# Four PSUM banks of two score tiles taken anew as four tiles of one bank, in an attention and MLP kernel

## The chip, the core and the metric

The kernel runs on one core of a Trainium2 chip. The metric is the device time of one execution in microseconds, and the median over several executions is compared. TensorE (PE, with its weight loads as PEld), VectorE (DVE), ScalarE (ACT), GpSimd (POOL) and SyncE (SP) each work through an instruction list of their own in order. They wait for each other on semaphores. TensorE writes its products to PSUM, which has eight banks; DVE and ACT read them from there.

## What is computed

Attention with RMS-normalised q and k, followed by an MLP over the tokens of all heads:

```python
# q, k, v: (8, 12, 448, 64); w_in: (768, 2048); w_out: (2048, 768)
q_n, k_n = rmsnorm(q, g_q), rmsnorm(k, g_k)
attn = softmax(q_n @ k_n^T / 8)
x = (attn @ v).transpose(0, 2, 1, 3).reshape(3584, 768)
h = x @ w_in
out = (h * sigmoid(1.702 * h)) @ w_out          # (3584, 768), float32
```

## The kernel before

**Attention.** A unit of work is a pair of heads of one batch: 6 pairs in each of 8 batches. `score` (L1170) multiplies k by q for a block of 112 keys into a score tile of PSUM; `expo` (L1178, L1180) takes the exponential on ACT; `values` (L1191) multiplies by v into a tile `o`; `divide` (L1201, L1202) normalises on DVE, and a transpose puts the result as columns of x into `xT`.

**PSUM.** Eight banks are shared out at the start. Two score tiles `sc0` and `sc1` have two banks each, one for each head of the pair, since one `exp` reads both. The tile `o` has one bank, and `w0`, `w1`, `w2` have one each. A list `banks` names what the matrix products may write to: places 0 to 2 are the `w` tiles, and places 3 to 6 are the single banks within the score tiles. These four lines make it (L1008 to L1010 and L1014):

```python
banks = [ps_w.tile([128, 512], FP32, tag=f"w{j}", name=f"w{j}") for j in range(3)]
sc_ring = [ps_sc.tile([128, 2, 512], FP32, tag=f"sc{j}", name=f"sc{j}") for j in range(2)]
banks += [t[:, j, :] for t in sc_ring for j in range(2)]
...
return banks[od.got]
```

**The MLP.** For batches 0 to 5, `first` (L1403) multiplies by `w_in`, `tanh` (L1413) and `gate` (L1425) make the activation, and the product with `w_out` follows (L1433 plain, L1497 in a form with seven products for every eight, whose operands are sums made on DVE at L1488). A product's result is taken out of PSUM by ACT (`copy_out`, L1507), or added to an earlier part by DVE (`add_out`, L1515). The first product of the last two batches is made jointly, again with seven products in place of eight: `joint_product` (L1744) writes three matmuls for each of the seven into a bank, ACT or DVE copies a part out (`part_copy`, L1755 and L1753), DVE adds later parts (`part_add`, L1758), and `gelu` (L1764) makes the activation on ACT. Its operand differences are made on DVE at L1728 and L1734.

**The order.** The kernel has no loop at run time. Every step is added to a planner (`_Order`) with an engine, an assumed duration, a key, the steps it depends on and the PSUM slot that it takes. The planner plays the steps through by these assumed durations and emits each engine's instructions in the order found. A slot named "w" stands for a place in `banks`; it has 3 places until the step "late" (L1842), which depends on the last `exp` and widens it to all 7. Steps with engine "none" emit no instruction of their own. Tile places and waits are made below this level: the waits between engines come from which tiles the instructions read and write.

Of the kernel before, what the change touches and what calls it, by code (L numbers as in the profile page):

```python
# [9 lines left out]
FP32 = mybir.dt.float32  # L10
# [5 lines left out]
PSUM = bass.MemoryType.PSUM  # L16
# [841 lines left out]
def kernel(  # L858
# [31 lines left out]
    def pool(name, bufs, **kw):  # L890
        return ctx.enter_context(tc.tile_pool(name=name, bufs=bufs, **kw))
# [43 lines left out]
    late = consts.tile([128, 3 * T_LEN + N_SUM * S_LEN], BF16, name="late", tag="late")  # L935
# [58 lines left out]
    for t in att_ring[1:]:  # L994
        flat = t[:, :, :, :].rearrange("p n h q -> p (n h q)").bitcast(FP32)
        osb_ring += [flat[:, j * S:(j + 1) * S] for j in range(NS)]
    ps_sc = pool("ps_sc", 1, space=PSUM)
    ps_o = pool("ps_o", 1, space=PSUM)
    ps_w = pool("ps_w", 1, space=PSUM)

    od = _Order()
    for name, n in (("sc", 2), ("o", 1), ("w", 2), ("th", 3), ("osb", 5)):
# [5 lines left out]
    banks = [ps_w.tile([128, 512], FP32, tag=f"w{j}", name=f"w{j}") for j in range(3)]  # L1008
    sc_ring = [ps_sc.tile([128, 2, 512], FP32, tag=f"sc{j}", name=f"sc{j}") for j in range(2)]
    banks += [t[:, j, :] for t in sc_ring for j in range(2)]  # L1010
    scored = [0]

    def bank():
        return banks[od.got]  # L1014
# [243 lines left out]
    def last_values(i):  # L1258

        return [("P", i, None, w, NS - 1) for w in range(2)] + [("P", i, h, 0, NS - 1)  # L1260
                                                                for h in range(2)]
# [8 lines left out]
    for i in range(NG):  # L1270
        b = i // NP
# [57 lines left out]
    for u in units:  # L1329
        i, h = u  # L1330
        b = i // NP
# [193 lines left out]
    def now_key():  # L1525
        return 10.3 + min(done, TURN) / PACE + max(done - TURN, 0.0) / PACE_2
# [198 lines left out]
    def w_term(j, h):  # L1725
        o, x, y, op = W_TERMS[j]
        o, x, y = (t[:, :, h * FH // 2:(h + 1) * FH // 2] for t in (o, x, y))
        nc.vector.tensor_tensor(out=o, in0=x, in1=y, op=op)  # L1728

    def x_term(j):  # L1730
        o, x, y = ((X1, x_half(B1, 0), x_half(B0, 0)),
                   (x_half(B1, 0), x_half(B1, 1), x_half(B1, 0)),
                   (X2, x_half(B1, 1), X1), (X4, x_half(B0, 1), X2))[j]
        nc.vector.tensor_tensor(out=o, in0=x, in1=y, op=ALU.subtract)  # L1734
# [79 lines left out]
    for b in range(B - 1):  # L1814
        bp = b // 2
        if b == B - 2:
            b = B - 1
# [19 lines left out]
        if b == B0 - 1:  # L1837
            od.add("keep", "DVE", 650, keep, now_key() + 0.5, lock=True,
                   deps=[("G", B0 - 2, m) for m in range(MI)]
                   + [x for p in range(NG - 2) for x in last_values(p)])  # L1840
            before_g.append("keep")
            od.add("late", "none", 0, lambda: None, 0, widen=[("w", len(banks))],  # L1842
                   deps=[("E", NG - 1, None, t) for t in range(NS)])
            od.add("later", "none", 0, lambda: None, 0,
                   widen=[("osb", len(osb_ring)), ("sums", len(sums))],
                   deps=last_values(NG - 1))
            for j in range(4):
                for h in range(2):
                    od.add(("WT", j, h), "DVE", 960, lambda j=j, h=h: w_term(j, h),
                           now_key() + 1.5 + j / 10, lock=True,  # L1850
                           deps=[last] + [("WT", i, h) for i in range(j)]
                           + [x for p in range(NG - K_RAW, NG)
                              for x in (("N", p, 0), ("N", p, 1), ("V", p))])
            for j, d in enumerate(((0, 1), (1,), (1,), (0,))):
                od.add(("XT", j), "DVE", 860, lambda j=j: x_term(j), now_key() + 2.0 + j / 10,
                       lock=True,
                       deps=[("XT", i) for i in range(j)]
                       + [("X", (B0 + e) * NP + p, None) for e in range(2) for p in range(NP)
                          if j or p < KH]
                       + [x for p in range(NG - K_RAW, NG)  # L1860
                          for x in (("N", p, 0), ("N", p, 1), ("V", p))])
# [73 lines left out]
```

## Time and profile before

| what | before |
|---|---|
| median of 4 runs | 424.08 us (423.62 to 426.0) |
| the profiled execution | 423.85 us |
| its span, first to last instruction | 422.1 us |
| PE busy | 404.8 us, 96% |
| DVE busy | 324.3 us, 77% |
| ACT busy | 295.4 us, 70% |
| POOL busy | 173.5 us, 41% |
| mean DMA rate | 150 GB/s |
| granted TensorE clock | 1.0 throughout |

The busy times are of one profiled execution, and all times within it count from the start of its span. Matmuls overlap: a row of three matmuls at L1744 reads 0.73 us, while the next group can start 0.57 us after it. So a stall on PE is read from the starts of neighbouring groups and not from the idle time between them. A trace names both banks of a score tile `sc`. In the timeline neighbouring instructions of one engine and line are merged ("x3"), and a bracket at the end of a row tells how long the engine had been idle and what ended it.

### The profile page before, as it was taken

The numbers are of one execution on the slowest core, as the hardware profiler recorded it, in microseconds if no ns is written. First come the engines' busy times: TensorE is split into PE (matmuls) and PEld (weight loads), VectorE is DVE, ScalarE is ACT, GpSimd is POOL, SyncE is SP. The second block draws the span as 40 slices with busy tenths as digits, with TensorE's granted clock in tenths as the row PEclk, the third lists the DMA queues.
The fourth block names the chain that finished last, engine by engine and source line by source line (L and its number), as shares of the span: only waits on it lengthen the run. The fifth ranks groups of instructions, "written<-read, shape, count | busy, mean of one in ns | idle before, by whom it ended". The sixth has DMA issues, their size and how long they took to land.

```text
span 422.1 us, 10002 instructions
## 1 busy us (share of the span) xinstructions
PE 404.8 (96%) x3845; PEld 237.6 (56%) x3845; DVE 324.3 (77%) x647; ACT 295.4 (70%) x435; POOL 173.5 (41%) x252
## 2 busy tenths in 40 slices
PE   7899989999999999999999999999999999999995
PEld 5568876555555555554555555555555654545663
DVE  4878888869999788888798869997666897557432
ACT  4898595989788578776896758858887625773221
POOL 4965887571726175809447363752300000000000
PEclk9999999999999999999999999999999999999999
DMA  8999999965394899695875879558351231001223
GB/s 214 254 245 245 259 249 248 242 171 130 78 191 119 187 206 227 121 230 132 205 174 119 196 182 231 122 111 181 93 110 36 74 77 43 3 0 27 87 76 112
DMA packets 101555, 63.38 MB, mean 150 GB/s; under 512 B 54916, under 2 KB 101508, under 8 KB 101508
## 3 DMA queue, kind: packets, MB, share of 16 engines
q1 hardware_dynamic: 93712, 55.88, 56.4%
q0 software_dynamic: 7296, 6.29, 9.1%
q8 instruction: 30, 0.49, 0.5%
q10 hardware_dynamic: 500, 0.57, 0.4%
q14 instruction: 17, 0.14, 0.1%
HBM read 45.61 MB, written 11.01 MB: 134 GB/s over the span
## 4 chain that ended last, share of the span: by engine, by line
PE 67%; DVE 13%; DMA 12%; ACT 3%; issue 2%; SPq 1%; POOL 0%; DVEq 0%; ACTq 0%; POOLq 0%
PE w L1403 19%; PE w L1497 18%; PE o L1191 9%; DMA rows<-in_v_dram 8%; PE sc L1170 8%; PE sc L1497 5%; PE w L1433 4%; DMA w_out_s<-in_moe_w_out_dram 3%; PE sc L1744 2%; DVE ssq L1058 2%; PE w L1744 2%; DVE late L1488 1%; DMA rows<-in_k_dram 1%; DVE obs L1202 1%; DVE att L1758 1%
## 5 line engine op out<-in xcount | busy, mean ns | idle before, releaser
L1178 ACT ACTIVATE att<-sc 112x896 bf16<-112x896 f32 x168 | 146.0, 917 | 35.7 <-PE sc L1170 35.0
L1403 PE MATMUL w<-xt,w_in_s 128*128 128x448 bf16 (+1 forms) x672 | 120.7, 326 | 0.6 <-DVE g L1425 0.4
L1403 PEld LDWEIGHTS <-w_in_s 128*128 128x128 bf16 x672 | 61.0, 98 | 44.6 <-issue 9.9
L1191 PEld LDWEIGHTS <-att 112*128 112x128 bf16 x1536 | 62.6, 98 | 29.8 <-issue 8.2
L1100 POOL TENSOR_TENSOR row<-rows,rs 112x512 bf16<-112x512 f32 x61 | 66.7, 1115 | 11.0 <-DMA qk<-row 9.1
L1413 ACT ACTIVATE th<-w 128x448 f32<-128x448 f32 x96 | 51.9, 548 | 23.4 <-PE w L1403 22.5
L1425 DVE SCALAR_TENSOR_TENSOR g<-th,w 128x448 bf16<-128x448 f32 x96 | 57.9, 615 | 12.9 <-ACT th L1413 12.6
L1058 DVE TENSOR_REDUCE ssq<-sq 112x16 f32<-112x1024 f32 (+1 forms) x50 | 58.3, 1170 | 10.0 <-ACT sq L1049 8.2
L1191 PE MATMUL o<-vx,att 112*128 112x65 bf16 x1280 | 58.8, 194 | 3.9 <-DVE obs L1202 3.0
L1113 POOL TENSOR_TENSOR vx<-rows,ones 112x512 bf16<-112x512 f32 x20 | 21.8, 1092 | 66.4 <-PE o L1191 58.6
L1170 PE MATMUL sc<-qk 64*128 64x448 bf16 (+1 forms) x360 | 47.3, 342 | 0.4 <-DVE qk L1130 0.2
L1046 POOL TENSOR_TENSOR sq<-rows 112x1024 f32<-112x1024 f32 (+1 forms) x14 | 26.8, 1914 | 42.1 <-DMA rows<-in_k_dram 18.8
L1202 DVE TENSOR_TENSOR obs<-o,rcp 112x256 bf16<-112x256 f32 x96 | 40.8, 425 | 3.3
L1497 PEld LDWEIGHTS <-g 128*128 128x128 bf16 x296 | 27.2, 98 | 21.1 <-issue 4.7
L1497 PEld LDWEIGHTS <-late 128*128 128x128 bf16 x304 | 27.5, 97 | 19.2 <-issue 2.9
L1049 ACT ACTIVATE sq<-rows 112x1024 f32<-112x1024 f32 (+1 forms) x32 | 32.4, 1018 | 6.8 <-DMA rows<-in_k_dram 4.1
L1497 PE MATMUL w<-w_out_s,g 128*128 128x384 bf16 x152 | 28.7, 326 | 0.0
L1497 PE MATMUL w<-w_out_s,late 128*128 128x384 bf16 x152 | 28.6, 326 | 0.0
L1201 DVE RECIPROCAL rcp<-o 112x4 f32<-112x4 f32 x96 | 17.0, 177 | 14.3 <-PE o L1191 14.0
L1497 PE MATMUL w<-late 128*128 128x384 bf16 x128 | 24.2, 326 | 0.1
L1100 DVE TENSOR_TENSOR row<-rows,rs 112x512 bf16<-112x512 f32 x27 | 22.5, 834 | 2.0 <-POOL rs L1093 2.0
L1180 ACT ACTIVATE att<-sc 112x896 bf16<-112x896 f32 x24 | 20.5, 917 | 1.4 <-PE sc L1170 1.3
(130 smaller groups left out, 503.5 us busy)
## 6 DMA issues: line engine op xcount, KB each, us to landing
rows<-in_q_dram SPq DMA_DIRECT2D x44, 224.0 KB, 4.6
rows<-in_k_dram SPq DMA_DIRECT2D x43, 224.0 KB, 4.7
rows<-in_v_dram SPq DMA_DIRECT2D x42, 224.0 KB, 3.5
w_in_s<-in_moe_w_in_dram POOLq DMA_DIRECT2D x4, 768.0 KB, 16.7
w_out_s<-in_moe_w_out_dram POOLq DMA_DIRECT2D x4, 768.0 KB, 20.8
out_dram<-osb SPq DMA_DIRECT2D x10, 168.0 KB, 3.4
out_dram<-osb SPq DMA_DIRECT2D x14, 120.0 KB, 2.2
out_dram<-osb SPq DMA_DIRECT2D x11, 144.0 KB, 2.5
```

The lines of the kernel that those rows point to most:

```text
L1046: nc.gpsimd.tensor_tensor(out=sq[i % N_SQ][:SS, part], in0=raw[turn(i, N_RAW, K_RAW)][:SS, part], in1=raw[turn(i, N_RAW, K_RAW)][:SS, part ...
L1049: nc.scalar.activation(out=sq[i % N_SQ][:SS, part], in_=raw[turn(i, N_RAW, K_RAW)][:SS, part], func=ACT.Square)
L1058: nc.vector.reduce_sum(out=ssq_of[g0][:SS, i - g0, part], in_=sq[i % N_SQ][:SS, part], axis=AX.X)
L1100: eng.tensor_tensor(out=row_ring[i % N_QKN][:SS, gi].rearrange("p n (h d) -> p h n d", h=2), in0=raw[turn(i, N_RAW, K_RAW)][:SS, gi], in1= ...
L1170: nc.tensor.matmul(sc[:, hp, j * SH:j * SH + n], lhsT=qkw[r, k0:k0 + WIN], rhs=qk[r, 0, qs], start=True, stop=True)
L1178: nc.scalar.activation(out=att[:SS, t, :, :S], in_=sc, func=ACT.Exp)
L1191: nc.tensor.matmul(os_[u, w][:, x, :], lhsT=att_of(u)[:SS, kc, hp, qs * SS:qs * SS + WIN], rhs=vx_ring[turn(i, N_V, K_V)][:SS, hp, kc, :], ...
L1202: nc.vector.tensor_tensor(out=to[:SS, :, w, :] if h is None else to[:SS, :2].rearrange("p n h d -> p (n h) d"), in0=o[:SS, :, :D], in1=rcp ...
L1403: nc.tensor.matmul(gps[b, m][:, j * SH:j * SH + n], lhsT=w_in_s[:, ki, f * 128:(f + 1) * 128], rhs=xT[b][:, ki, lo:lo + n], start=(ki == 0 ...
L1413: nc.scalar.activation(out=th[:, :], in_=gps[b, m][:, :S], func=ACT.Tanh, scale=0.851)
L1425: nc.vector.scalar_tensor_tensor(out=g_of[b // 2][:, f:f + len(g), lo:lo + n], in0=view(ths.pop((b, m))[:, :]), scalar=1.0, in1=view(gps.p ...
L1497: nc.tensor.matmul(held[to], lhsT=lhs[:, ko, :], rhs=y[:, ko, :], start=first and ko == 0, stop=ko == NK - 1, skip_group_check=not first)
```

## The change

The pool of the score tiles is opened in a stack of its own, after the pools of `o` and `w` rather than ahead of them. At the step "late", the one that widens "w", this stack is closed. A new pool then takes four tiles of one bank each, which become places 3 to 6 of `banks`. The sizes, the number of places and the planner's steps, keys and durations stay.

```diff
@@ -994,9 +994,10 @@
-    ps_sc = pool("ps_sc", 1, space=PSUM)
     ps_o = pool("ps_o", 1, space=PSUM)
     ps_w = pool("ps_w", 1, space=PSUM)
+    scores = ctx.enter_context(ExitStack())
+    ps_sc = scores.enter_context(tc.tile_pool(name="ps_sc", bufs=1, space=PSUM))
@@ -1009,6 +1010,11 @@
     sc_ring = [ps_sc.tile([128, 2, 512], FP32, tag=f"sc{j}", name=f"sc{j}") for j in range(2)]
     banks += [t[:, j, :] for t in sc_ring for j in range(2)]
     scored = [0]
+
+    def part_banks():
+        scores.close()
+        ps_b = pool("ps_b", 1, space=PSUM)
+        banks[3:] = [ps_b.tile([128, 512], FP32, tag=f"b{j}", name=f"b{j}") for j in range(4)]
@@ -1839,7 +1845,7 @@
-            od.add("late", "none", 0, lambda: None, 0, widen=[("w", len(banks))],
+            od.add("late", "none", 0, part_banks, 0, widen=[("w", len(banks))],
                    deps=[("E", NG - 1, None, t) for t in range(NS)])
```

## The prediction

> **What bounds the kernel now.** I read first the page's busy times, then the chain that ended last, then busy time by stretch, and last the timeline of the one stretch in which the four banks of the change are used. The page says that TensorE is the engine that sets the time.
>
> ```profile
> span 422.1 us, 10002 instructions
> PE 404.8 (96%) x3845; PEld 237.6 (56%) x3845; DVE 324.3 (77%) x647; ACT 295.4 (70%) x435; POOL 173.5 (41%) x252
> PE 67%; DVE 13%; DMA 12%; ACT 3%; issue 2%; SPq 1%; POOL 0%; DVEq 0%; ACTq 0%; POOLq 0%
> ```
>
> The change can only touch work that uses `banks[3:]`. These are taken once the planner widens the slot "w" at the end of attention, so almost all of it lies in the joint product of the last two batches (L1744) and in the closing products (L1497). I cut the span there:
>
> ```profile
> 0.00:349.70 349.70, 337.69 (x3468) 200.87 (x3469) 287.68 (x586) 264.38 (x373) 173.51 (x252) 1.00 0.77 171
> 349.70:383.00 33.30, 32.63 (x168) 16.28 (x167) 19.56 (x34) 22.84 (x46) 0.00 (x0) 1.00 0.02 7
> 383.00:422.10 39.10, 34.49 (x212) 20.44 (x209) 17.10 (x29) 8.15 (x17) 0.00 (x0) 1.00 0.29 82
> ```
>
> The columns are the stretch, its length, the busy time of PE, PEld, DVE, ACT and POOL, the granted clock, the DMA share and GB/s. In the middle row DVE (19.56 of 33.30) and ACT (22.84) have room, DMA is idle (0.02) and the clock is whole: PE waits there only for hand-overs. The chain goes through ACT and DVE at just those places. In the timeline of the stretch they look like this (start, length, engine, line, what):
>
> ```profile
> 363.50 0.73 PE L1744 MATMUL sc<-rows,w_in_s 128*128 128x448 bf16 x3
> 364.07 0.73 PE L1744 MATMUL w<-rows 128*128 128x448 bf16 x3
> 364.33 0.51 ACT L1755 COPY att<-sc 128x448 f32<-128x448 f32 x1
> 364.90 0.73 PE L1744 MATMUL sc<-rows,w_in_s 128*128 128x448 bf16 x3
> ...
> 369.43 1.30 PE L1744 MATMUL sc<-xt,w_in_s 128*128 128x448 bf16 x6
> 370.26 0.53 ACT L1755 COPY att<-sc 128x448 f32<-128x448 f32 x1
> 370.84 0.73 PE L1744 MATMUL sc<-xt,rows 128*128 128x448 bf16 x3
> ```
>
> Three matmuls at full rate start the next group 0.57 us later (363.50 to 364.07). From 364.07 to 364.90 it is 0.83: a stall of 0.26 us. The group at 364.90 starts 0.05 after ACT's copy has ended (364.33 + 0.51 = 364.84). From 369.43 six matmuls should take 1.13, but 370.84 is 1.41 later: 0.28 lost, again 0.05 after an ACT copy out of `sc`.
>
> **The change part by part.** First what it does not do. Set beside each other, the two built programs have the same instructions in the same order on all five engines: 7691 rows on PE, and the same on the others. Only waits differ, and no difference lies before 342 us of the span; between 342 and 349.7 one PE wait goes, whose source had ended at 343.07, 0.7 us before the matmul could start. So nothing is moved past a queue, no DMA is added, and giving back and taking anew costs no instruction. The first matmul into a new tile (336.8 us) waits for the last `exp` out of an old one, as before; that `exp` ended at 335.0, so this costs nothing and would begin to cost only if it ended 1.8 us later.
>
> What changes is the grain of the waits. With one tile over two banks, a matmul into one bank waits for a read of the other, and a copy out of one bank waits for matmuls into the other. I went through every PE stall of 349.7 to 383 and asked which wait is in the new program. Each loss is the step between starts, less the step at full rate (0.189 us per 448-column matmul, 0.162 per 384-column one).
>
> - 349.93, the group into `sc`: lost 0.23, waiting for DVE's L1515 out of the other bank (ends 349.88). The wait goes, but the next group (350.49) still needs DVE's copy L1753, which ends 350.41 and is not hurried by this. Gain only 0.03.
> - 352.47: lost 0.27, behind ACT's copy of 351.88 to 352.41. That wait stays, but the copy itself had waited for the group at 351.06 in the other bank; its own bank was finished one group (0.57) earlier. The copy moves up 0.57, the stall is gone: 0.27.
> - 358.40: lost 0.27, behind ACT's copy of 357.82 out of the other bank. In its place comes a wait for the DVE add of 356.26, which ends 356.88, over 1.2 us before it is needed: 0.26.
> - 364.90: lost 0.26. As at 352.47, with one link more: the ACT copy stands behind a gelu that waits for the DVE add at 363.19, which waited for a group in the other bank of its tile and is free 0.57 sooner. All three move up together: 0.26.
> - 370.84: lost 0.27, as at 358.40: 0.27.
> - 377.35: lost 0.28, as at 364.90: 0.28.
> - 378.01: lost 0.09 behind the DVE add that follows this same copy; it goes with it: 0.09.
> - 382.74, the fifth matmul of L1497 after 381.86: lost 0.23 behind DVE's add of 382.06 to 382.68 out of the other bank. The wait goes and nothing replaces it: 0.23.
>
> The sum is 0.03 + 0.27 + 0.26 + 0.26 + 0.27 + 0.28 + 0.09 + 0.23 = 1.69 us. About 0.28 us more is lost at 380.63 and 381.29, on hand-overs out of `w` and within one bank; these waits are in the new program too.
>
> After 383 PE runs without a pause at 0.162 per matmul except for one 0.15 us stall at 390.0 (an ACT copy out of a `w` bank, unchanged), so the whole gain is carried to the last matmul. Behind it stand ACT's last copy (417.53), its store (issued 418.05) and the landing, some 4 us, which move up as a block. The waits that the change takes off PE after 383 were not binding: their sources had ended 0.5 us or more before.
>
> New waits cost nothing while they have cover. About ten PE groups now name the true earlier reader of their bank in place of a reader of the neighbour. The tightest is the group at 358.40 with 1.2 us of cover, and behind a late one there would queue all of PE. The 24 adds of L1758 (0.62 each) and 16 copies of L1755 (0.53 each) follow PE and move with it.
>
> [...] By the busy row PE is idle 33.30 - 32.63 = 0.67 us in the stretch, so one would put the gain at 0.67 at most. [...] I take the steps: 1.69 rather than 0.67.
>
> [...]
>
> The sum stands against the profiled execution: 422.1 of span, 423.85 with what lies around it, so 422.16. The median of the four runs is 0.23 above that execution: 424.08 - 1.69 = **422.4 us**, or 0.40% less.
>
> **The rivals.**
>
> *The gain is larger.* All steps lost in 349.7 to 383 add up to 0.23 + 0.27 + 0.27 + 0.26 + 0.27 + 0.28 + 0.09 + 0.28 + 0.23 = 2.18 us. If the moved ACT and DVE work also freed the `w` hand-overs, the time would be 421.9. Against it: their waits are true data waits that hang on PE's own groups.
>
> *The gain is given back.* Here each group freed runs into the next hand-over: with PE ahead, the DVE add or ACT copy of the same bank comes last. DVE and ACT are 59% and 69% busy in the stretch, and ACT often runs four operations in a row. If half of the freed stalls come back, the time is 424.08 - 0.85 = 423.2; if all do, or the change doesn't bind at all, 424.1. For it: at 350.49 just this happens. Against it: the covers of 1.2 us.
>
> *The time ends higher.* The score pool is now taken after the others, so scores, `o` and `w` lie in other banks through all of attention. If reading or writing depended on which bank it is, the 192 `exp` of 917 ns and the matmuls would change. PE is 67% of the chain, 283 us: matmul steps longer by 0.6% would eat the whole gain, and by 1.35% (3.8 us) make it over 0.5% slower, 426.2 or more. Against it: copies of L1755 out of `w` and out of `sc` both take 532 ns, and matmuls of L1744 into `w` and into `sc` both have a median of 352 ns.
>
> **How the numbers follow.** The bound of what can be told from no change is about 0.5%, 2.12 us. The forecast gets 0.69, the larger gain 0.12, the gain given back 0.13, the higher time 0.06. The four runs spread over 2.4 us, so a median is good to some 0.8 us; with 1.69 expected and the edge at 2.12, about three in ten of the forecast's cases fall beyond the edge. Faster by over 0.5%: 0.69 x 0.3 + 0.12 = 0.33. Slower: 0.06. Same: 0.61. The range goes from 421.2 (the larger gain and a low median) to 424.2 (all given back). The forecast's own range is 421.5 to 423.3.
>
> **What would show it right or wrong.** Right: no `sc` group in the joint stretch, but `b` tiles; between 350 and 383 the steps behind L1755 copies fall from 0.83 to 0.57 for three matmuls; the stretch from the start of the first group after 350 to the last joint matmul is shorter by about 1.4 us, and the first 340 us agree within the noise of two executions. Wrong: stalls of 0.1 to 0.3 us in front of new groups, released by DVE adds; or any difference that has grown before 340 us, which would speak for the banks' place and not for the waits.

## The result, and the profile after

| what | before | after |
|---|---|---|
| median | 424.46 us (64 runs, 421.57 to 427.51) | 423.07 us (43 runs, 420.33 to 424.55) |
| ratio of the times, with its 95% interval | | 0.9962 (0.9949 to 0.9974) |
| the profiled execution, and its span | 423.85, 422.1 us | 423.98, 422.2 us |

The changed kernel is faster by 0.38%. The forecast was 0.40%, so 1.69 us of 424. The difference is real, as the interval leaves out 1, and smaller than the 0.5% that the prediction took as the bound. The two profiled executions don't show it: their spans are 422.1 and 422.2 us. That is the first thing to clear up. The page of the changed kernel, the same rows as shown before (the span, the busy times, the shares of the chain that ended last):

```profile
span 422.2 us, 10002 instructions
PE 404.7 (96%) x3845; PEld 238.4 (56%) x3845; DVE 323.8 (77%) x647; ACT 295.7 (70%) x435; POOL 173.3 (41%) x252
PE 67%; DMA 19%; DVE 9%; issue 2%; POOL 2%; ACT 1%; SPq 0%; POOLq 0%; DVEq 0%; ACTq 0%
```

PE's work is the same to 0.1 us. On the chain, DVE fell from 13 to 9% and ACT from 3 to 1%, and DMA rose from 12 to 19%. The rise of DMA belongs to the first 90 us of the kernel. From 349.7 to 383 us the chain is now PE but for 0.3%, where PE had 52% of it before. The same three stretches as before (length, busy time of PE, PEld, DVE, ACT and POOL with the number of instructions, clock, DMA share, GB/s):

```profile
0.00:349.70 349.70, 336.87 (x3460) 200.83 (x3461) 285.56 (x584) 264.55 (x373) 173.34 (x252) 1.00 0.77 170
349.70:383.00 33.30, 33.21 (x176) 17.03 (x175) 20.77 (x36) 22.75 (x45) 0.00 (x0) 1.00 0.06 17
383.00:422.20 39.20, 34.65 (x213) 20.54 (x210) 17.49 (x30) 8.44 (x17) 0.00 (x0) 0.99 0.29 81
```

In the middle row PE starts 176 matmuls in the 33.30 us, where it was 168 before. In the first row it is 8 matmuls behind (3460 against 3468): this execution came to the joint product late and made it up there.

To keep the two apart I measure a stretch between the same two instructions in every profile: from the start of the first joint matmul to the start of the last matmul of the kernel. It is worked out from the starts of the TensorE rows. A joint group is the three matmuls of L1744 (L1750 in the changed kernel) that go into one bank one after the other; the fifth one starts at 349.13 us before. Each column counts from the mark of the column to its left.

| | first joint matmul | to the fifth joint group | to the fifth matmul of the closing product (L1497) behind the last joint one | to the last matmul | the stretch |
|---|---|---|---|---|---|
| before | 341.71 us | 7.42 | 33.60 | 34.43 | 75.45 |
| after | 343.55 us | 7.42 | 31.93 | 34.44 | 73.78 |

The joint product gives 1.67 us, all of it between its fifth group and its end, and the closing part carries it to the end unchanged. The front took 1.84 us from the same execution. In the timeline of the changed kernel (start, length, engine, line; the numbers of lines are 6 higher than before), this is what has become of the two stalls shown before, at 364.90 and 370.84:

```profile
364.78 0.73 PE L1750 MATMUL b<-rows,w_in_s 128*128 128x448 bf16 x3
365.04 0.52 ACT L1761 COPY att<-b 128x448 f32<-128x448 f32 x1
365.34 0.73 PE L1750 MATMUL w<-rows 128*128 128x448 bf16 x3
365.91 0.73 PE L1750 MATMUL b<-rows,w_in_s 128*128 128x448 bf16 x3
...
370.45 1.30 PE L1750 MATMUL b<-xt,w_in_s 128*128 128x448 bf16 x6
371.57 0.53 ACT L1761 COPY att<-b 128x448 f32<-128x448 f32 x1 [0.33 <-ACT g L1770]
371.59 0.73 PE L1750 MATMUL b<-xt,rows 128*128 128x448 bf16 x3
```

From 365.34 to 365.91 it is 0.57 us, where it was 0.83. ACT's copy starts 0.26 after the group at 364.78, where before it started 0.83 after the like group at 363.50: 0.57 sooner, by one group, as forecast. At 371.59 PE starts 1.14 after 370.45, where it was 1.41, although ACT's copy began only 0.02 us before it: the copy reads another bank, and the wait for it is gone.

Now the front. The same 8 us of the span, first before, then after (columns as above):

```profile
8.00:16.00 8.00, 5.98 (x77) 4.49 (x78) 6.24 (x14) 5.92 (x10) 6.75 (x8) 1.00 1.12 261
```

```profile
8.00:16.00 8.00, 5.91 (x62) 4.26 (x62) 5.40 (x12) 4.85 (x9) 6.45 (x8) 0.79 1.13 232
```

PE got through 62 matmuls in place of 77, at a granted clock of 0.79 in place of 1.00. The clock record of this execution has TensorE at half speed from 11.64 to 15.05 us. No wait and no order differs there between the two programs. Counted by matmuls, the changed kernel was 0.40 us behind before that spell (the 41st matmul), 1.28 behind after it (the 151st) and 1.84 behind at the joint product, so at most about half of it came in the spell. Whether the changed places of the banks had a part in this is what the first experiment asks.

### The profile page after: what moved, and what is told of

It reads as the page before. It is cut to its first block, busy times and chain, and to the rows that moved or that the text cites. A ratio compares the mean times of both kernels' runs of the same rounds, so it can differ in the third digit from the quotient of the medians.

```text
span 422.2 us, 10002 instructions
## 1 busy us (share of the span) xinstructions
PE 404.7 (96%) x3845; PEld 238.4 (56%) x3845; DVE 323.8 (77%) x647; ACT 295.7 (70%) x435; POOL 173.3 (41%) x252
## 4 chain that ended last, share of the span: by engine, by line
PE 67%; DMA 19%; DVE 9%; issue 2%; POOL 2%; ACT 1%; SPq 0%; POOLq 0%; DVEq 0%; ACTq 0%
PE w L1409 19%; PE w L1503 18%; PE o L1197 9%; PE sc L1176 7%; DMA rows<-in_k_dram 6%; DMA w_out_s<-in_moe_w_out_dram 6%; PE b L1503 5%; PE b L1750 4%; DMA late<-in_v_dram 4%; PE w L1750 4%; DMA late<-in_k_dram 2%; PE w L1439 2%; DMA rows<-in_q_dram 1%; DVE late L1494 1%; DVE obs L1208 1%
```

## The experiments

Theory: the gain is the grain of the waits, 1.69 us in the joint product and nothing elsewhere. Rivals: part of the freed time is given back to the next hand-over; the other places of the banks cost something in attention.

**The order of the pools alone.** The kernel before, with the score pool taken last as in the change, and its two tiles kept to the end.

```diff
-    ps_sc = pool("ps_sc", 1, space=PSUM)
     ps_o = pool("ps_o", 1, space=PSUM)
     ps_w = pool("ps_w", 1, space=PSUM)
+    ps_sc = pool("ps_sc", 1, space=PSUM)
```

> Only the place of the pools is changed: the score pool is opened after those of o and w, so scores, o and w lie in other banks through all of attention, and the two score tiles stay whole to the end. By the theory of the waits (a tile of two banks ties two unrelated products together) nothing changes: the stretch from the first joint matmul to the last matmul stays at 75.45 us as in the kernel before, and the time is that of the kernel before within 0.2%. By the rival of the banks' place, part of the 1.6 us is here: the stretch becomes 74.6 or less, or the time moves by 0.3% or more either way.

Measured: 423.89 us (12 runs) beside 424.02 of before, ratio 1.0005 (0.9981 to 1.003). The stretch is 75.45 us, that of before, and the first joint matmul starts at 341.40 us (341.71 before). The places of the banks cost nothing that can be seen; that rival falls, and with it the reading that the late front of the one profile came from them.

**One score tile parted at a time.** In the changed kernel, one of the two tiles stays in a pool that is never closed, and only the other's two banks are taken anew.

```diff
+    ps_kept = pool("ps_kept", 1, space=PSUM)
...
-    sc_ring = [ps_sc.tile([128, 2, 512], FP32, tag=f"sc{j}", name=f"sc{j}") for j in range(2)]
+    sc_ring = [(ps_sc if j == 0 else ps_kept).tile([128, 2, 512], FP32, tag=f"sc{j}", name=f"sc{j}")
+               for j in range(2)]
...
-        banks[3:] = [ps_b.tile([128, 512], FP32, tag=f"b{j}", name=f"b{j}") for j in range(4)]
+        banks[3:5] = [ps_b.tile([128, 512], FP32, tag=f"b{j}", name=f"b{j}") for j in range(2)]
```

This is the first tile parted; for the second it reads `j == 1` and `banks[5:7]`.

> Only sc0 is given back and taken anew as two tiles of one bank; sc1 stays one tile of two banks. By the theory of the waits only the stall at 349.93 goes, and only 0.03 us of it is kept, since the next group waits for the same VectorE copy as before. At 364.90 and 377.35 two waits stand one behind the other, one on each tile, and freeing one of them brings nothing. So the stretch from the first joint matmul to the last is 75.4 us (0.03 less than 75.45). If the gain went with the number of banks parted, it would be half, 74.6.

> Only sc1 is parted. By the theory the stalls at 352.47, 358.40, 370.84 and 382.74 go (0.27, 0.26, 0.27, 0.23), and those at 364.90 and 377.35 stay but for 0.04 each, because their ScalarE copy still stands behind a gelu that waits for a group in the other bank of sc0. Sum 1.1: the stretch is 74.35 us, 0.25% of the time. The two halves then add up to 1.13, and not to the 1.67 of both together. If each stall hung on one tile alone, sc1 would give all but 0.03 of it, 73.8.

Measured: with the first tile parted the stretch is 75.41 us (0.04 less than before) and the time 423.67 (ratio 1.0014, 0.999 to 1.0038). With the second parted it is 74.44 (1.01 less) and 424.29 us (1.0007, 0.9981 to 1.0033). The second time is a miss: 1.01 us would be a ratio of 0.9976, just outside its interval. Why the shorter stretch doesn't show in these 12 runs is open; the profile of this kernel, too, reaches the joint product late (344.16 us). So what follows rests on the stretches, of one profile each. The parts add up to 1.05 us, and both together give 1.67. The 0.62 that is over belongs to places where both tiles must be parted. The timeline of the first experiment shows one of them, the stall that stood at 364.90 before:

```profile
363.74 0.73 PE L1752 MATMUL w<-rows 128*128 128x448 bf16 x3
363.98 0.53 ACT L1763 COPY att<-sc 128x448 f32<-128x448 f32 x1 [0.46 <-PE sc L1752]
364.56 0.73 PE L1752 MATMUL sc<-rows,w_in_s 128*128 128x448 bf16 x3
```

ACT's copy waits for a group into the other bank of the tile that was kept, and the step is 0.82. In the timeline of the second, the same place:

```profile
365.77 0.58 ACT L1772 ACTIVATE g<-att 128x448 bf16<-128x448 f32 x1 [1.32 <-DVE att L1766]
365.99 0.73 PE L1752 MATMUL w<-rows 128*128 128x448 bf16 x3
366.25 0.51 ACT L1763 COPY att<-b 128x448 f32<-128x448 f32 x1
366.82 0.73 PE L1752 MATMUL b<-rows,w_in_s 128*128 128x448 bf16 x3
```

Here the copy reads a bank of its own, and the step is still 0.83: the copy stands behind the gelu of 365.77, and this waited 1.32 us for a DVE add out of the tile that was kept. These are the two links that the prediction named for 364.90 and 377.35. With the 0.09 at 378.01 that hangs on the latter they come to 0.26 + 0.28 + 0.09 = 0.63, which is the 0.62 that neither part gives alone.

**How much cover the new waits have.** The changed kernel, with the DVE add that the group of product 3 waits for (`part_add` with j = 3, five times; J22 in the texts below) done once, twice or three times more into a tile that nothing reads.

```diff
+    spare = obs[0][:, :, :, :].rearrange("p n h d -> p (n h d)")[:, :S]
+
     def part_add(n, j, to):
+        for _ in range(2 if j == 3 and n < 5 else 0):
+            nc.vector.tensor_tensor(out=spare, in0=joint[n, to][:, :S], in1=part_of[n, j], op=ALU.add)
```

> The changed kernel, with the VectorE add J22 of the joint groups n = 0 to 4 done three times over, twice into a tile that nobody reads. By the profile of the change its result lies there 1.34 to 1.4 us before the TensorE group that waits for it. Two extra adds of 0.62 us are 1.25 us: by the theory of covers they cost nothing and the stretch stays at 73.78 within 0.1. By the rival (a freed group runs into the next hand-over at once) the stretch grows by 1 us or more, some 0.25 us or more for each of the five groups.

> The same with three extra adds, 1.87 us, which is 0.5 us more than the cover. Theory: TensorE now waits at each of the five groups, so the stretch grows by 1.5 to 3 us, to between 75.3 and 76.8, and the groups behind the add start 0.05 us after its end. If the stretch stays at 73.8, the cover is larger than it was read.

Measured: two more adds make the stretch 79.20 us (5.42 more than the changed kernel; one run, 429.21 us), three make it 82.50 (8.72 more; one run, 430.62). Both expectations were missed: the first theory had 73.78 and the second 76.8 at most. The rival of the first, a growth of 1 us or more, is what came. The cover of 1.2 us that the prediction gave is not there. So I asked what one more add does, with a new theory: the add is late for ACT before it is late for PE.

> One extra VectorE add of 0.62 us ahead of J22 for n = 0 to 4 in the changed kernel. The run with two extra adds grew by 5.4 us, and the waits found there lie not at the group that reads J22's bank but at a later one that waits for a ScalarE copy, which had stood behind the gelu of J22. New theory: the cover is what this copy has in the profile of the change: 0.30, 0.31, 0.31, 0.29 and 0.02 us for the five groups. One add of 0.62 us then costs 0.32 + 0.31 + 0.31 + 0.33 + 0.60 = 1.9 us, and the stretch is 75.6 (75.2 to 76.0). If the cover of 1.34 us read at VectorE's own wait were the true one and the two extra adds had met another limit, the stretch stays at 73.8.

Measured: 75.88 us, 2.10 more (one run, 425.13 us). Five adds of 0.66 us each from start to start are 3.3 us of DVE; the second and third set of five cost 3.32 and 3.30, all of it, and the first 2.10. The timeline of the kernel with one more add shows the way (L1767 is the unread add, L1768 the real one):

```profile
361.50 0.62 DVE L1767 TENSOR_TENSOR obs<-b,osb 128x448 bf16<-128x448 f32 x1 [0.53 <-ACT osb L1761]
362.16 0.62 DVE L1768 TENSOR_TENSOR osb<-b,osb 128x448 f32<-128x448 f32 x1
362.82 0.58 ACT L1774 ACTIVATE g<-osb 128x448 bf16<-128x448 f32 x1 [0.87 <-DVE osb L1768]
363.30 0.52 ACT L1774 ACTIVATE g<-w 128x448 bf16<-128x448 f32 x1
363.73 0.52 ACT L1761 COPY att<-w 128x448 f32<-128x448 f32 x1
364.28 0.62 DVE L1768 TENSOR_TENSOR att<-b,att 128x448 f32<-128x448 f32 x1 [0.96 <-ACT att L1761]
364.94 0.58 ACT L1774 ACTIVATE g<-att 128x448 bf16<-128x448 f32 x1 [0.69 <-DVE att L1768]
365.42 0.51 ACT L1761 COPY att<-b 128x448 f32<-128x448 f32 x1
365.99 0.73 PE L1750 MATMUL b<-rows,w_in_s 128*128 128x448 bf16 x3 [0.34 <-ACT att L1761]
```

Read it downwards: the add of 362.16 is late, the gelu that needs it waits (0.87), the next gelu and the copy of 363.73 stand behind it on ACT, the DVE add of 364.28 waits for that copy (0.96), the next gelu for that add (0.69), the copy of 365.42 stands behind that gelu, and PE at last waits for the copy. None of the five groups that wait for the delayed add itself lost anything. In the changed kernel, shown above, the copy answering to that of 365.42 ends at 365.56 and PE takes the bank at 365.91; less the 0.05 of a hand-over, 0.30 us of cover. At the five places it is 0.30, 0.31, 0.31, 0.29 and 0.02 us, 1.23 together, and 3.3 - 1.23 = 2.07 is near the 2.10. The single places don't follow this sum: the first lost 0.13 us and the other four 0.49 each, where 0.66 - 0.30 is 0.36. All five losses stand before a PE group that waits for an ACT copy, and the rows show the way at one of them; the agreement of the sum may be chance.

With two more adds the add's own group waits too, 0.28 us at four of the five places; the text on the one extra add, above, has that wrong. With three more it loses another 0.66 there. In the timeline of the kernel with three:

```profile
368.85 1.94 DVE L1767 TENSOR_TENSOR obs<-w,att 128x448 bf16<-128x448 f32 x3 [0.53 <-ACT att L1761]
370.83 0.62 DVE L1768 TENSOR_TENSOR att<-w,att 128x448 f32<-128x448 f32 x1
371.50 0.35 PE L1750 MATMUL w<-xt,rows 128*128 128x448 bf16 x1 [0.77 <-DVE att L1768]
```

**The stalls that are left.** Ahead of the fifth joint group the changed kernel still loses 0.66 us at 348.34. In its timeline:

```profile
347.73 0.55 DVE L1521 SCALAR_TENSOR_TENSOR att<-b,att 128x384 f32<-128x384 f32 x1
348.34 1.46 PE L1503 MATMUL b<-w_out_s,sq 128*128 128x384 bf16 x8 [0.50 <-DVE att L1521]
```

PE waits for DVE's L1521, which stands behind three operand differences of L1734, 0.95 us each. Three of the differences (terms, in the texts below) are not needed so early. This kernel gives them due times of their own.

```diff
 AT = {
+    ('WT', 1, 1): 349500, ('WT', 2, 1): 352000, ('WT', 3, 1): 358000,
```

> On top of the change, three VectorE terms of the weights' second half (0.95 us each, first needed at n = 4) may not start in the planner before 349.5, 352 and 358 us in place of 339 to 346. Theory: in the profile of the change PE loses 0.66 us before the L1503 group at 348.34, 0.20 before the joint group at 350.40 and 0.19 at 352.06, all behind a VectorE queue that is full up to there. With two terms (1.9 us) taken out ahead of these adds most of the three losses goes: the stretch falls from 73.78 to between 72.8 and 73.1 us, and the time is 0.6% below the kernel before. Rival: the terms land among the adds of the joint groups and make PE wait there, whose cover is 1.2 us, or the other true waits take over: the stretch is 73.6 or more.

Measured: 421.81 us (12 runs), ratio to before 0.9949 (0.9925 to 0.9973), and a stretch of 72.83 us: 0.95 less than the changed kernel, 0.76 of it ahead of the fifth joint group. The planner also moved one copy from ACT to DVE in this kernel. In its timeline:

```profile
346.73 0.56 DVE L1522 SCALAR_TENSOR_TENSOR att<-b,att 128x384 f32<-128x384 f32 x1
346.74 1.46 PE L1504 MATMUL w<-late,g 128*128 128x384 bf16 x8
...
348.04 1.47 PE L1504 MATMUL b<-w_out_s,sq 128*128 128x384 bf16 x8
```

DVE's read of the bank starts with the group ahead and not behind it, and PE goes from one group to the next in 1.30 us, 8 times 0.162.

Does this gain need the parted banks? The same three due times in the kernel before:

> The kernel before, score tiles left whole, with the three late weight terms of the run before this one. If the two gains are independent, the stretch from the first joint matmul to the last falls from 75.45 us by the 0.95 us that the late terms gave on top of the change, to 74.5. If the late terms only pay once the banks are parted, it stays above 75.

Measured: a stretch of 75.20 us, 0.25 less than before, in one run (425.65 us beside 424.42). Ahead of the fifth joint group it gains the same 0.76 (6.66 against 7.42), but the joint product then takes 34.11 us in place of 33.60. In its timeline:

```profile
352.70 0.73 PE L1745 MATMUL w<-rows 128*128 128x448 bf16 x3
352.96 0.53 ACT L1756 COPY att<-sc 128x448 f32<-128x448 f32 x1 [1.17 <-PE sc L1745]
353.54 0.73 PE L1745 MATMUL sc<-rows,w_in_s 128*128 128x448 bf16 x3
```

A step of 0.84, the stall between the two banks of one tile as before. Late differences leave more such stalls there, so the edit is worth 0.25 us with the tiles whole and 0.95 with them parted. The two gains are not independent. The two kernels with late differences have the same instructions in the same order on every engine in their profiles, and only the tiles `sc` and `b` differ. Step by step the one with whole tiles falls behind at nine places, by 0.09 to 0.33 us each, and by 2.37 us in all (75.20 against 72.83). So in this order parting the banks is worth 2.37 us, where it was worth 1.67 in the old one.

**Both once more, on one chip.** The changed kernel as it is, and the one with late differences.

> The changed kernel once more, beside the version with late terms on the same chip: 0.9962 of the kernel before, with an interval of some 0.25%, and a stretch of 73.78 us.

> The change with the late weight terms once more. The stretch is 72.83 us again, 0.95 less than with the change alone, so the time is to be 0.22% below that of the change beside it and about 0.6% below the kernel before.

Measured beside 424.96 us of before: 422.65 (9 runs; 0.9939, 0.9913 to 0.9965) and 421.39 (6 runs; 0.992, 0.9889 to 0.9951). The stretches are 73.77 and 72.82 us, those of the first profiles to 0.01. This profile of the changed kernel has no spell of half clock: its first joint matmul starts at 341.04 us and its span is 419.7 us, where the first had 343.55 and 422.2. The kernel with late differences is 0.30% below the changed one by the medians, where its stretch says 0.22%. Against the kernel before it is faster beyond the interval; against the changed one only the stretch shows it, in both pairs of profiles, as 9 and 6 runs that spread over some 4 and 3 us can't tell 0.3%.

## Why the prediction was right

- **The mechanism and the sum held.** 1.67 us of the stretch against 1.69 forecast. Followed group by group, the changed kernel's lag of 1.84 us behind the kernel before fell to 1.80, 1.53, 1.27, 1.02, 0.75, 0.48 and 0.16: 0.04 at 349.93 (forecast 0.03), 0.27 at 352.47 (0.27), 0.26 at 358.40 (0.26), 0.26 at 364.90 (0.26), 0.27 at 370.84 (0.27), 0.27 at 377.35 (0.28) and 0.32 for the last two (0.09 + 0.23). Of the small one at 349.93 the prediction said that the next group's wait for DVE's copy would eat the rest, and it does.
- **The stalls with two links held.** They are what each parted tile alone can't remove: 0.62 us against 0.63.
- **Steps and not busy time.** Busy time allowed 0.67 us at most. The stall of 0.26 us at 364.90 stands there as 0.10 us of idle: the row ahead ends at 364.80 (364.07 + 0.73), while the step is 0.83. In the middle stretch PE's busy time rose by 0.58 us, while 1.67 were gained.
- **Whole tiles and not banks.** The old waits were of the grain of a tile: before, the six matmuls at 357.00 and the next group are 1.40 us apart, behind ACT's copy out of the other bank, and in the changed kernel the same step is 1.14 (358.53 to 359.67). Had they been by bank already, nothing would have come of it.
- **The time.** 422.4 us was made from a median of four runs, 424.08; before's median over 64 runs is 424.46. The forecast's 0.40% of it is 422.77; the measured ratio makes it 422.85, and the median of the changed kernel is 423.07. These differences are smaller than the noise of such medians, so nothing more can be read from them.
- **The rival of the places of the banks** fell by the order of the pools alone (1.0005, and the same stretch).
- **What failed: "the covers of 1.2 us".** The prediction said that the tightest of the new waits was the group at 358.40, with 1.2 us of cover. For that one hand-over it was about right, but it isn't the tightest, and it was the wrong thing to look at. It counted the wait between DVE and PE alone. The nearest edge goes through ACT's order, and there the cover read from the profile is 0.02 to 0.31 us. The gain given back, which got 0.13, was nearer than the text said: one more add of 0.66 us at each of five places takes the whole gain (2.10 against 1.67). It didn't come, as the change puts no work on DVE or ACT; but the argument that the prediction held against it was wrong, and that it had the right side of this rival was in part luck.
- **What also failed: "the first 340 us agree within the noise of two executions".** They differed by 1.84 us, and by the prediction's own test that spoke for the places of the banks. The test was badly made: one pair of executions differs by that much without any edit (341.04 and 343.55 for the changed kernel itself).

## What to carry to other kernels

When two halves of one PSUM tile are used as independent buffers, look at which releaser the waits name: here a tile of two banks cost 1.67 us in 33, and the stalls could be added up one by one from the steps between matmul starts. For an edit below half a per cent, measure between the same two instructions of the critical engine in both profiles; here that repeated to 0.01 us, where the span of one kernel moved by 2.5. Before calling a wait covered, follow the late instruction through every engine that runs in order behind it, since cover to the next wait of PE (1.2 us and more here) says nothing of what stands behind it on ACT (0.02 to 0.31 us).

## What the runs showed of the hardware

Half-clock spells come in 5 of the 12 profiles: the mean granted clock is 0.993 to 0.995 in these, and 0.998 or more in the other seven. The two spells that the views show whole are 3.41 us at 0.50, from 11.64 to 15.05 us in the changed kernel's profile and from 10.85 to 14.26 us in the first with late differences. The changes of clock seen here fall on a grid of that length counted from the first full grant: in the changed kernel's profile they come 6.83, 10.24 and 416.43 us behind the grant of 4.81 us, which is 2, 3 and 122 lengths; in the first with late differences the spell starts 6.83 us behind (4.02 to 10.85), and with the second tile parted and with two more adds 58.02 us (6.35 to 64.37 and 5.14 to 63.16), 2 and 17 lengths. In the changed kernel's profile the window ahead of the spell, and the spell, are (columns as above):

```profile
8.22:11.64 3.42, 1.64 (x15) 1.04 (x15) 2.79 (x7) 1.11 (x3) 2.57 (x3) 1.00 1.14 231
11.64:15.05 3.41, 3.32 (x31) 2.52 (x31) 2.00 (x4) 3.16 (x6) 2.71 (x4) 0.50 1.13 232
```

PE was busy for 1.64 us of the window ahead of the spell, and the longest single gap that reaches into it is 1.87 us (7.35 to 9.22). In the five windows on this grid that a spell follows PE was busy 1.21, 1.30, 1.52, 1.64 and 1.67 us, 35 to 49% of them. Of the other windows at full clock that end before the last matmul does, none in the profiles of before and after has under 2.12 us; the least that a view of another profile shows is 1.86 us (one more add, 60.38 to 63.80).

So under half of the window was busy ahead of each spell here; that this is the cause, no run shows. That share is no sure sign either. At the end of the kernel with the first tile parted there is a window with 1.46 us of PE, and full clock behind it:

```profile
415.69:419.10 3.41, 1.46 (x10) 0.68 (x7) 0.56 (x1) 0.49 (x1) 0.00 (x0) 1.00 0.53 152
419.10:421.70 2.60, 0.00 (x0) 0.00 (x0) 0.00 (x0) 0.00 (x0) 0.00 (x0) 1.00 0.08 28
```

The first full grant comes at 4.02 to 7.20 us, so the grid falls differently from run to run. In the second profile of the changed kernel it comes at 6.75 us; the four windows from there to 20.40 us have 2.65, 2.82, 2.70 and 3.23 us of PE, and there is no spell. No run here moved the idle time or the grid on purpose, so why the same kernel has a spell in one profile and none in the next is not shown. Ahead of that grant the clock has no record and a view shows 1.00, but in the profiles of before and of after the 256-column matmuls start 0.21 us apart there and 0.11 us apart behind it. So in these two PE runs at about half rate until then, and the clock of 1.0 in the table of the kernel before holds from 5.73 us on.

A spell can cost at most half its length of matmul time, 1.7 us, by an estimate from its 3.41 us at 0.50. The five profiles with one are those of the changed kernel, of the second tile parted, of two more adds, and both of the changed kernel with late differences. They reach the first joint matmul at 343.26 to 344.16 us; of the seven without, five do so at 341.04 to 341.71, one at 342.51 and one at 343.77. So the spells go with a later front, but they are not all of it.
